# Marks in the model of a hand-planned order: the moves that hold a mark stop overwriting one another

## Chip, cores and metric

The kernel runs on one core of a Trainium2 chip. The metric is the device time of one execution in microseconds (us), the median of several runs.

## What is computed

Causal attention with a decay, for 8 batches of 8 heads with 576 positions and 64 columns per head, and then a two-layer MLP with a Mish gate over the 4608 tokens. Cut to what matters:

```
scores = q @ k.T / sqrt(64) + cum[:, None] - cum[None, :]    # cum = cumsum(log(clip(f)))
scores = where(causal, -1e9, scores)
attn   = softmax(scores) @ v                                 # (8, 8, 576, 64)
x      = attn as 4608 tokens x 512
h      = x @ w_in                                            # 512 -> 2048
out    = (h * tanh(softplus(h))) @ w_out                     # 2048 -> 512
```

## The kernel before

Every float32 value is carried as two float16 parts, high and low, and a product is made of several float16 products. The attention runs over 32 pairs of heads, g = 0 to 31, four pairs to a batch. The MLP runs over 9 chunks of 512 tokens; a chunk can start when the pairs of its batch are done. The weights are loaded as raw words and converted and split on the vector and scalar engines while the first pairs run.

For each pair g, `prep(g)` (line 1060) scales q and k, splits them into a tile `hl` with four parts (pairs 1 and 3 use a piece of `xa[1]` for it, line 1076), and issues DMAs that build the operand tile `ST1`. Two of them, one for t = 0 (the query side) and one for t = 1 (the key side), copy three rows for each of the two heads out of `cumd`, a DRAM tensor with the cumulative sums of the decay (line 1087); in the trace they are `st<-cumd`. They write different rows, D + 3t to D + 3t + 2, and different halves of the tile. Two more copy the high parts of q and k (line 1090); in the trace `st<-hl`, or `st<-xa` for pairs 1 and 3. `prep2(g)` (line 1094) fills the second operand tile `ST2` with four more copies of the same name. `max_items(g)` (line 1142) makes the scores a first time and takes row maxima with vector reductions into `mx`; `st_items(g)` makes them again for the exponentials.

Nothing is issued in the order in which the Python code runs. `Program.choose` (line 188) only records each operation, with the regions that it reads (`r`) and writes (`w`). `deps` (line 305) turns overlaps into a dependency graph: a write depends on earlier reads and writes of the region that it overlaps, a read on earlier writes. `schedule` (line 365) then runs a list scheduler with a cost model forward and backward ten times in all, replays each of the ten orders with four draws of random delays, and keeps the order with the lowest mean end. Some operations may go to one of several engines; the scheduler chooses (`choose` with several ways). `emit` writes each engine's instructions in that order. The real waits between engines are put in afterwards, from the tiles that the instructions touch, so the graph decides the order and the engines, not the synchronisation.

Beside true regions the graph has pretended ones. A *mark* is a pretended write: while `nc.mark` is set, each recorded operation also "writes" the region named by it. A *gate* is a pretended read: an operation recorded while `nc.gate` is set "reads" that region, and so comes after the operations that hold the mark. The marks are `rows0` to `rows3`, held by the two `st<-cumd` moves of pairs 0 to 3 (line 1085, `NSEL = 4`), and `sums`, held by the first store of `cumd` (line 796). The gates are `rows0` on the loads of all weights (line 883) and of the first batch of v (line 1795), and `rows2` on the second batch of v (line 1802). The q and k loads of pairs 2 and 3 carry the gate `rows0` as well (line 1764), but they are recorded ahead of the marks, so the marked moves come after them. In the model a DMA's successor becomes ready some 1.6 us after its issue cost, plus its bytes and a margin of 0.3 us (lines 592 to 596), and the SP queue, which issues nearly all DMAs, is held when the modelled backlog grows too long (line 523).

All marked moves write the same region of their mark:

```
if self.gate:
    r.append((self.gate, 0, 1, 0, 1))
if self.mark:
    w.append((self.mark, 0, 1, 0, 1))
```

The scheduler also fills some waits of the tensor engine with matmuls of no use, to keep its clock up (`warmed`, line 335); in the trace they are `b<-idm,idh`.

Of the kernel before, what the change touches and what calls it, by code (L numbers as in the profile page):

```python
# [27 lines left out]
S = 576  # L28
D = 64
# [100 lines left out]
BACK = 4000  # L130
LOOK = dict(zip(('tensor', 'vector', 'scalar', 'gpsimd', 'sync'), (float(x) for x in ("0", "0", "0", "0", "0",))))
PRIO = 200
MARGIN = dict(tensor=100,vector=100,scalar=100,gpsimd=0,sync=300)
DRAWS = 4
WORK, LAGS, MOVES = 0.02, 50.0, 300.0
# [25 lines left out]
class Program:  # L161
# [26 lines left out]
    def choose(self, *ways):  # L188

        r, w, opts = [], [], []  # L190
        for way in ways:
            total, port = 0.0, False
            for eng, method, a, kw in way:
                aps = [(k, x) for k, x in list(enumerate(a)) + list(kw.items()) if hasattr(x, "tensor")]
                w += [z for k, x in aps if k in ("out", "accum_out", 0) for z in self.region(x)]
                r += [z for k, x in aps if k not in ("out", "accum_out", 0) for z in self.region(x)]
                if eng == "scalar":
                    (r if method == "activation" else w).append(("table", 0, 1, 0, 1))
                if eng == "tensor":

                    w.append((w[0][0] + "/pe", 0, 1, 0, 1))
                port |= self.shared(eng, method, aps)
                cost = self.cost(eng, method, kw, aps)
                if isinstance(cost, tuple) and total:

                    total = (total[0] + 8, total[1] + cost[1], 0)
                else:
                    total = cost if isinstance(cost, tuple) else total + cost + (80 if total else 0)
            opts.append((eng, way, total, port))
        if self.gate:  # L210
            r.append((self.gate, 0, 1, 0, 1))
        if self.mark:
            w.append((self.mark, 0, 1, 0, 1))
        key = len(self.ops)
        if self.rank is not None:
            key, self.rank[1] = self.rank[0] + self.rank[1], self.rank[1] + self.rank[2]
        self.ops.append((opts, r, w, key))
        self.leads.append(self.lead)
        self.forms.append(self.form(*ways[0][0]) if ways[0][0][0] == "tensor" else None)
        func = ways[0][0][3].get("func") if ways[0][0][0] == "scalar" and len(ways) == 1 else None  # L220
        self.sets.append("mish" if func == AF.Mish else "exp" if func == AF.Exp else None)
        if self.sets[-1] and self.phase is not None:
            n = len(self.sets)
            w.append((f"phase{self.phase}", 0, 1, n, n + 1))
            r.append((f"phase{self.phase - 1}", 0, 1, 0, 1 << 30))

        self.banks.append({
            x.tensor.name for _, _, a, kw in ways[0] for x in list(a) + list(kw.values())
            if hasattr(x, "tensor") and x.space == PSUM})
# [248 lines left out]
    def forward(self, deps, succ, rank):  # L478
# [43 lines left out]
        while len(order) < n:  # L522
# [69 lines left out]
            if way[0][1].startswith("dma_start"):  # L592
                hw = max(t, hw) + cost[0]
                clock[q] = t + 50
                dma = max(dma, hw + 650) + cost[1]
                end, own = dma + 930 + MARGIN["sync"], 0.0
            else:
# [17 lines left out]
                clock[q] = t + cost  # L615
                end, own = clock[q], self.DELAY[q] + MARGIN[q]
            ends[i] = end
# [28 lines left out]
def scaled_rest(out, in_, scale, hi, e):  # L646

    if e == "vector":
        return [(e, "scalar_tensor_tensor", (), dict(
            out=out, in0=in_, scalar=scale, in1=hi, op0=ALU.mult, op1=ALU.subtract))]  # L650
    return scaled(in_, in_, scale, e) + sub(out, in_, hi, e)
# [32 lines left out]
def attn_moe(ctx: ExitStack, tc: tile.TileContext, qk, v, f, w_in, w_out, out):  # L684
    nc = Program(tc.nc)
# [26 lines left out]
        out=msk, in_=msk, pattern=[[-1, P]], compare_op=ALU.is_ge, fill=-60000.0,  # L712
# [4 lines left out]
    for j in range(2):  # L717
        nc.gpsimd.affine_select(
            out=msk2[j * D : (j + 1) * D], in_=msk2[j * D : (j + 1) * D], pattern=[[-1, D]],
# [14 lines left out]
    for j in range(2):  # L734
        r = slice(j * D, (j + 1) * D)
# [7 lines left out]
    ST1 = [cp.tile([P, 2, 2, S], F16, name=f"st1_{i}") for i in range(NST)]  # L743
    ST2 = [cp.tile([P, 2, 2, S], F16, name=f"st2_{i}") for i in range(NST2)]
# [3 lines left out]
    for t, first, fills in ((0, 0.0, ((KM - 4, -1.0), (KM - 1, 0.0))), (1, 1.0, ((KM - 4, 0.0), (MROW, -MSC), (KM, 0.0)))):  # L748
        nc.gpsimd.memset(rowv[:, t], first)
        for row, x in fills:  # L750
            nc.gpsimd.affine_select(
                out=rowv[:, t], in_=rowv[:, t], pattern=[[0, 2]], compare_op=ALU.is_ge, fill=x,
# [23 lines left out]
    def flat(t):  # L776
        return t[0:BH].rearrange("p j t s -> p (j t s)")

    tmp = [flat(ST2[i]).bitcast(F32)[:, S * j : S * (j + 1)] for i in (1, 0) for j in range(2)]
    ft = tmp[0]  # L780

    def decay():
        _, on, cm, r1 = tmp
        nc.vector.memset(on, 1.0)
        nc.vector.tensor_scalar(out=ft, in0=ft, scalar1=1e-4, scalar2=1.0, op0=ALU.max, op1=ALU.min)
        nc.scalar.activation(out=ft, in_=ft, func=AF.Ln)
        nc.scalar.preload_act_table_set("exp_and_others")
        nc.vector.tensor_tensor_scan(
            out=cm, data0=on, data1=ft, initial=0.0, op0=ALU.mult, op1=ALU.add)
        c = flat(ST2[1])[:, 0 : 3 * S].rearrange("p (r s) -> p r s", r=3)  # L790
        nc.vector.tensor_scalar(out=c[:, 0], in0=cm, scalar1=8.0, scalar2=None, op0=ALU.mult)
        nc.vector.scalar_tensor_tensor(
            out=r1, in0=cm, scalar=8.0, in1=c[:, 0], op0=ALU.mult, op1=ALU.subtract)
        nc.vector.tensor_copy(out=c[:, 1], in_=r1)
        nc.vector.tensor_tensor(out=c[:, 2], in0=r1, in1=c[:, 1], op=ALU.subtract)
        nc.mark = "sums"
        for h in (slice(0, H), slice(H, BH)):
            nc.mark = None if h.start else "sums"
            nc.sync.dma_start(out=cumd[h], in_=c[h])
        nc.mark = None  # L800
# [20 lines left out]
    def square_sum(o, x, scale=1.0):  # L821
        junk = sp.tile([P, S], BF16, name="junk", tag="junk", bufs=1)
        nc.scalar.activation(
            out=junk[:, 0 : x.shape[-1]], in_=x, func=AF.Square, scale=scale, accum_out=o)
# [232 lines left out]
    def place1(g):  # L1057
        return g % NST if g < NB else (g - NB + ((NB - 1) % NST == 0)) % 2

    def prep(g):  # L1060
        b, p = divmod(g, NP)
        x = st[g]["qk"]
        i = place1(g)
        am = sp.tile([P, 2], F32, name=f"qa{g}", tag="qa", bufs=4)
        for j in range(2):
            square_sum(am[:, j : j + 1], x[:, j])
        t = sp.tile([P, 2], F32, name=f"qt{g}", tag="qt", bufs=4)
        ami, ti = am.bitcast(I32), t.bitcast(I32)
        nc.vector.tensor_tensor(out=ti[:, 0:1], in0=ami[:, 1:2], in1=ami[:, 0:1], op=ALU.subtract)
        nc.vector.tensor_scalar(  # L1070
            out=ti[:, 0:1], in0=ti[:, 0:1], scalar1=0.25, scalar2=float(127 << 23), op0=ALU.mult, op1=ALU.add)
        nc.vector.tensor_scalar(
            out=ti[:, 0:1], in0=ti[:, 0:1], scalar1=EXPMASK, scalar2=None, op0=ALU.bitwise_and)
        nc.vector.reciprocal(out=t[:, 1:2], in_=t[:, 0:1])
        if g in (1, 3):
            hl = xa[1].rearrange("p a h n -> p (a h n)")[:, 0 : 4 * S].rearrange("p (t s) -> p t s", t=4)
        else:
            hl = sp.tile([P, 4, S], F16, name=f"hl{g}", tag="hl", bufs=NHL)
        for j, (hi, lo) in enumerate(((1, 3), (2, 0))):
            nc.choose(*(scaled(hl[:, hi], x[:, j], t[:, j : j + 1], e) for e in SV))  # L1080
            nc.choose(*(scaled_rest(hl[:, lo], x[:, j], t[:, j : j + 1], hl[:, hi], e) for e in (
                ("vector", "gpsimd") if AO & 2 else ("gpsimd",) if j < (HL2 if g < HLP else HL3) else ("vector",))))
        st[g]["hl"] = hl
        h0 = b * H + 2 * p
        nc.mark = f"rows{g}" if g < NSEL else None
        for t in range(2):
            nc.sync.dma_start(out=ST1[i][D + 3 * t : D + 3 * t + 3, :, t], in_=cumd[h0 : h0 + 2].rearrange("h r s -> r h s"))
        nc.mark = None
        for j in range(2):
            nc.sync.dma_start(out=ST1[i][0:D, j], in_=hl[j * D : (j + 1) * D, 1:3])  # L1090
        if NSEL <= g < NB and g - NST >= NSEL:
            nc.sync.dma_start(out=ST1[i][MROW : MROW + 1, :, 0], in_=zrow[0:1])
# [35 lines left out]
    def beside(*products):  # L1128
# [8 lines left out]
        out=sel, in0=idm[:, 0:9].unsqueeze(2).to_broadcast([P, 9, P]), scalar1=-MSC / 1024.0, scalar2=None,  # L1137
# [610 lines left out]
    def ranked(rank, f):  # L1748
# [8 lines left out]
        out=psum(RB)[:, 0:DN], lhsT=idh, rhs=idm.unsqueeze(1).to_broadcast([P, DN // P, P]), start=True, stop=True))]  # L1757
# [143 lines left out]
    for t0, t1 in zip([0] + TB, TB):  # L1901
        now = [place[x, t - x * W1] for t in range(t0, t1) for x in range(2) if 0 <= t - x * W1 < NF]
        for i in now:
            r = KS0 + i * KSS
# [92 lines left out]
```

## Time and profile before

| what | value |
|---|---|
| median of 3 runs | 1014.1 us (1013.09 to 1015.46) |
| the profiled execution: its own time | 1014.29 us |
| the profiled execution: span, first to last instruction | 1012.6 us |
| mean granted clock of the tensor engine | 0.993 |
| tensor engine busy | 978.1 us (97%) |
| vector engine busy | 731.1 us (72%) |
| scalar engine busy | 728.9 us (72%) |

A share over the whole span is a mean over stages with different limits, so it is read together with a table of the stages. In the trace all recorded operations have one line, 333, since one helper emits them; they are told apart by the names of their tiles. SPq is the queue of the engine SP that issues DMAs; PE is the tensor engine, PEld its weight loads, DVE the vector engine, ACT the scalar engine, POOL GpSimd.

### The profile page before, as it was taken

How to read it: one execution, taken by the hardware profiler on the slowest of the kernel's cores; microseconds unless marked ns; L12 is line 12 of the kernel's file. 1: busy time of each engine (PE TensorE's matmuls, PEld its weight loads, DVE VectorE, ACT ScalarE, POOL GpSimd, SP SyncE). 2: the span in 40 equal slices, each digit the busy share in tenths (PEclk: the TensorE clock that was granted, in tenths of full speed). 3: DMA queues.
4: the chain of work that ended last, by engine and by line, in shares of the span. 5: the costliest groups of instructions: out<-in, count | busy, mean ns of one | idle time of the engine just before them, and what ended most of it. 6: DMA issues, size and time to landing. Idle time of an engine off the chain costs nothing.

```text
span 1012.6 us, 20652 instructions
## 1 busy us (share of the span) xinstructions
PE 978.1 (97%) x7663; PEld 544.1 (54%) x7663; DVE 731.1 (72%) x2002; ACT 728.9 (72%) x1421; POOL 10.4 (1%) x65
## 2 busy tenths in 40 slices
PE   4999899998999999999999999999999999999998
PEld 4788445544554554555455555455555555656664
DVE  7999999986677776776666766776766669953432
ACT  6668999978778777777778877787886665524323
POOL 2000000000000000000000000000000000000000
PEclk8999999999999999999999999999999999999999
DMA  6999974779777857687868766786775432001001
GB/s 198 324 266 244 262 169 108 154 173 187 158 145 160 173 127 153 136 180 145 142 141 179 148 146 142 170 158 115 138 152 112 70 75 72 4 1 42 1 1 42
DMA packets 256446, 139.57 MB, mean 138 GB/s; under 512 B 226650, under 2 KB 227034, under 8 KB 256346
## 3 DMA queue, kind: packets, MB, share of 16 engines
q1 hardware_dynamic: 256346, 138.26, 61.7%
q8 instruction: 60, 0.98, 0.4%
q14 instruction: 40, 0.33, 0.1%
HBM read 45.68 MB, written 9.66 MB: 55 GB/s over the span
## 4 chain that ended last, share of the span: by engine, by line
PE 65%; DVE 16%; ACT 7%; DMA 6%; issue 3%; SPq 1%; POOL 0%; DVEq 0%; ACTq 0%; POOLq 0%
PE b L333 65%; DVE wall L333 3%; DVE b L333 2%; DMA pt<-hb 2%; DMA st<-hl 2%; SPq L333 1%; ACT junk L333 1%; DVE hl L333 1%; DVE hb L333 1%; ACT st L333 1%; ACT hb L333 1%; DMA out_dram<-ot 1%; DVE gl L333 1%; DVE x L333 1%; ACT more_e L333 1%
## 5 line engine op out<-in xcount | busy, mean ns | idle before, releaser
L333 PEld LDWEIGHTS <-wall 128*128 128x128 f16 x3372 | 322.3, 98 | 357.9 <-issue 24.0
L333 PE MATMUL b<-gh,wall 128*128 128x512 f16 x1152 | 366.5, 380 | 0.0
L333 PE MATMUL b<-xa,wall 128*128 128x512 f16 (+1 forms) x1602 | 345.0, 366 | 8.3 <-ACT me L333 4.6
L333 PE MATMUL b<-gl,wall 128*128 128x512 f16 x576 | 218.2, 379 | 0.6 <-DVE gl L333 0.6
L333 PE MATMUL b<-st 70*128 70x512 f16 (+11 forms) x918 | 139.1, 285 | 13.7 <-DMA st<-cumd 6.9
L333 DVE SCALAR_TENSOR_TENSOR gl<-me,gsc,gh 128x512 f16<-128x512 f32 x144 | 106.3, 748 | 32.6 <-ACT gh L333 31.7
L333 ACT ACTIVATE me<-b,cinv 128x512 f32<-128x512 f32 (+1 forms) x130 | 85.0, 660 | 56.6 <-PE b L333 55.7
L333 PEld LDWEIGHTS <-st 70*128 70x128 f16 (+3 forms) x1110 | 87.3, 102 | 63.6 <-issue 18.7
L333 PE MATMUL b<-vv,pt 128*128 128x65 f16 (+5 forms) x2548 | 111.7, 203 | 1.1 <-DMA pt<-hb 0.7
L333 DVE CUSTOM_DVE_ANT_0 b<-b,mskw 128x256 f32<-128x256 f32 (+2 forms) x162 | 91.6, 567 | 9.9 <-PE b L333 8.8
L333 ACT ACT_TABLE_LOAD x70 | 89.8, 1283 | 1.2
L333 PEld LDWEIGHTS <-pt 128*128 128x128 f16 (+1 forms) x2268 | 70.9, 101 | 19.3 <-DMA pt<-hb 2.3
L333 ACT ACTIVATE st<-b,mn 128x512 f32<-128x512 f32 (+3 forms) x120 | 62.1, 548 | 22.7 <-DVE mn L333 19.4
L333 DVE TENSOR_TENSOR hb<-st,hb 128x512 f16<-128x512 f32 x81 | 55.8, 689 | 29.6 <-ACT hb L333 29.1
L333 DVE TENSOR_TENSOR hb<-more_e,hb 128x512 f16<-128x512 f32 x81 | 55.5, 689 | 29.6 <-ACT hb L333 29.3
L333 ACT ACTIVATE more_e<-b,mn 128x512 f32<-128x512 f32 (+3 forms) x123 | 62.4, 539 | 17.3 <-DVE mn L333 15.8
L333 DVE TENSOR_SCALAR gh<-me,gsc 128x512 f16<-128x512 f32 x66 | 31.9, 483 | 45.2 <-ACT me L333 44.3
L333 ACT ACTIVATE gh<-me,gsc 128x512 f16<-128x512 f32 x78 | 55.8, 720 | 1.8
L333 ACT ACTIVATE hb<-more_e 128x512 f16<-128x512 f32 x81 | 50.1, 627 | 9.5 <-DMA pt<-hb 8.8
L333 ACT ACTIVATE hb<-st 128x512 f16<-128x512 f32 x81 | 50.2, 627 | 7.6 <-DMA pt<-hb 5.6
L333 DVE TENSOR_TENSOR me<-b,hb 128x256 f32<-128x256 f32 x42 | 17.5, 422 | 50.5 <-PE b L333 49.9
L333 ACT ACTIVATE junk<-qk 128x576 bf16<-128x576 f32 x60 | 40.8, 680 | 15.5 <-DMA qk<-in_qk_dram 14.8
(173 smaller groups left out, 1005.3 us busy)
## 6 DMA issues: line engine op xcount, KB each, us to landing
st<-hl SPq DMA_DIRECT2D x180, 144.0 KB
qk<-in_qk_dram SPq DMA_DIRECT2D x30, 576.0 KB
v<-in_v_dram SPq DMA_DIRECT2D x32, 288.0 KB
out_dram<-ot SPq DMA_DIRECT2D x36, 256.0 KB
wall<-in_w_in_dram SPq DMA_DIRECT2D x16, 512.0 KB
wall<-in_w_out_dram SPq DMA_DIRECT2D x16, 512.0 KB
pt<-hb SPq DMA_TRANSPOSE x162
st<-xa SPq DMA_DIRECT2D x12, 144.0 KB
```

Source lines behind the costliest of these rows:

```text
L333: r = getattr(real[eng], method)(*a, **kw)
```

## The change

A marked operation now writes a piece of the mark's region of its own, numbered by the operation, and a gated one reads the whole of it. So the operations that hold one mark no longer overlap: the t = 1 move of a pair no longer depends, in the model, on the t = 0 move. A gated operation still depends on every move that holds the mark and was recorded ahead of it, and a marked move still depends on gated loads recorded ahead of it. The rest of the diff has no effect as it stands: `NEAR` is 0, so the new branch is never taken, and `splits` is a view that was made in `decay` before. The recorded operations are the same.

```
+NEAR = 0
...
         if self.gate:
-            r.append((self.gate, 0, 1, 0, 1))
+            r.append((self.gate, 0, 1, 0, 1 << 30))
         if self.mark:
-            w.append((self.mark, 0, 1, 0, 1))
+            w.append((self.mark, 0, 1, len(self.ops), len(self.ops) + 1))
...
+    splits = flat(ST2[1])[:, 0 : 3 * S].rearrange("p (r s) -> p r s", r=3)
...
-        c = flat(ST2[1])[:, 0 : 3 * S].rearrange("p (r s) -> p r s", r=3)
+        c = splits
...
+            if g < NEAR:
+                for j in range(2):
+                    nc.sync.dma_start(out=ST1[i][D + 3 * t : D + 3 * t + 3, j, t], in_=splits[h0 + j : h0 + j + 1])
+                continue
```

## Rows read from the trace of the kernel before

**Rows 1.** The page's first part: busy time, share of the span and number of instructions of two engines.

```profile
PE 978.1 (97%) x7663; PEld 544.1 (54%) x7663; DVE 731.1 (72%) x2002; ACT 728.9 (72%) x1421; POOL 10.4 (1%) x65
```

**Rows 2.** Busy time by stage: the stretch in us, its length, then each engine's busy time and instructions, the granted clock of the tensor engine, the busy share of the DMA engines, and GB/s.

```profile
10.00:18.50 8.50, 1.57 (x29) 1.50 (x26) 6.75 (x24) 5.89 (x14) 0.00 (x0) 0.80 0.45 107
18.50:32.50 14.00, 10.68 (x93) 7.78 (x92) 10.70 (x27) 6.76 (x13) 0.00 (x0) 0.76 0.91 261
32.50:100.00 67.50, 66.12 (x743) 56.01 (x742) 66.62 (x191) 49.99 (x125) 1.05 (x5) 1.00 1.00 277
100.00:200.00 100.00, 94.89 (x702) 48.58 (x701) 99.02 (x287) 97.53 (x174) 0.81 (x4) 0.98 0.75 174
200.00:1000.00 800.00, 790.55 (x5999) 421.09 (x5997) 539.23 (x1463) 557.13 (x1078) 3.05 (x22) 1.00 0.58 119
1000.00:1012.60 12.60, 8.88 (x42) 3.82 (x39) 0.75 (x1) 3.18 (x5) 0.00 (x0) 0.96 0.22 83
```

**Rows 3.** The timeline of PE: start, length, operation, how many were merged, and in brackets the idle time before it with what ended it.

```profile
7.71 3.87 PE L333 MATMUL b<-idm,idh 128*128 128x128 f16 x62
18.51 0.27 PE L333 MATMUL b<-st 128*128 128x128 f16 x1 [6.94 <-DMA st<-cumd]
...
23.11 0.22 PE L333 MATMUL b<-st 128*128 128x128 f16 x1 [0.57 <-DVE mx L333]
...
27.95 0.23 PE L333 MATMUL b<-st 128*128 128x128 f16 x1 [1.87 <-DMA st<-xa]
```

**Rows 4.** The timeline of PEld: the first weight load of a score.

```profile
16.11 0.10 PEld L333 LDWEIGHTS <-st 128*128 128x128 f16 x1 [4.72 <-DMA st<-cumd]
```

**Rows 5.** The timeline of the SP queue from 12.5 us: start, length, the DMA that is issued.

```profile
12.99 1.13 SPq L333 DMA_DIRECT2D st<-hl  x2
14.22 1.05 SPq L333 DMA_DIRECT2D st<-cumd  x3
15.37 1.12 SPq L333 DMA_DIRECT2D st<-hl  x2
16.53 0.46 SPq L333 DMA_DIRECT2D st<-cumd  x1
17.03 1.88 SPq L333 DMA_DIRECT2D st<-hl  x2
18.96 0.46 SPq L333 DMA_DIRECT2D st<-cumd  x1
19.53 0.46 SPq L333 DMA_DIRECT2D st<-xa  x1
20.03 2.03 SPq L333 DMA_DIRECT2D v<-in_v_dram  x4
22.11 3.07 SPq L333 DMA_DIRECT2D st<-xa  x5
25.22 0.47 SPq L333 DMA_DIRECT2D st<-cumd  x1
26.05 1.62 SPq L333 DMA_DIRECT2D st<-hl  x2
27.92 1.88 SPq L333 DMA_DIRECT2D wall<-in_w_in_dram  x4
```

**Rows 6.** The same timeline asked for a narrow stretch (14.67 to 15.3 us): the second and the third of the three `st<-cumd` that are merged at 14.22.

```profile
14.67 0.60 SPq L333 DMA_DIRECT2D st<-cumd  x2
```

**Rows 7.** The timeline of DVE between 16 and 33 us.

```profile
16.65 1.55 DVE L333 SCALAR_TENSOR_TENSOR xa<-qk,qt,xa 128x576 f16<-128x576 f32 x2
19.56 1.35 DVE L333 TENSOR_REDUCE mx<-b 128x4 f32<-128x512 f32 x3 [1.36 <-PE b L333]
...
28.08 0.16 DVE L333 TENSOR_REDUCE am_m<-vc 128x1 f32<-128x4 f32 x1 [1.38 <-ACT junk L333]
...
32.45 0.42 DVE L333 TENSOR_SCALAR wall<-wall 128x512 int32<-128x512 int32 x1
```

**Rows 8.** The timeline of ACT.

```profile
20.63 1.44 ACT L333 ACTIVATE hl<-xa,qt 128x576 f16<-128x576 f32 x2 [4.01 <-DMA st<-hl]
23.21 0.68 ACT L333 ACTIVATE junk<-v 128x576 bf16<-128x576 f32 x1 [1.15 <-DMA v<-in_v_dram]
...
27.27 0.68 ACT L333 ACTIVATE junk<-v 128x576 bf16<-128x576 f32 x1 [0.43 <-DMA v<-in_v_dram]
```

**Rows 9.** The chain that ended last, in order of time: start, length, what the time went to.

```profile
22.11 5.80 DMA st<-xa
```

**Rows 10.** Busy time by stage again, for three stretches of the opening (columns as in rows 2).

```profile
14.50:18.50 4.00, 0.00 (x0) 0.10 (x1) 2.72 (x8) 1.52 (x3) 0.00 (x0) 0.57 0.67 153
18.50:22.50 4.00, 3.99 (x31) 2.98 (x30) 2.42 (x5) 1.44 (x2) 0.00 (x0) 0.58 0.68 171
22.50:32.50 10.00, 6.69 (x63) 4.80 (x62) 8.29 (x23) 5.32 (x11) 0.00 (x0) 0.83 1.00 297
```

**Rows 11.** Waits of PE from 100 us to the end: who waited for whom, us in total, times, the longest.

```profile
PE b L333 <- ACT me L333: 4.6, 5, 1.4
PE b L333 <- ACT st L333: 4.0, 7, 1.6
PE b L333 <- ACT more_e L333: 2.3, 3, 1.5
```

**Rows 12.** The page's costliest groups: operation and number | busy us, mean ns of one | idle before it. These are operations for which the scheduler may choose the engine.

```profile
L333 DVE SCALAR_TENSOR_TENSOR gl<-me,gsc,gh 128x512 f16<-128x512 f32 x144 | 106.3, 748 | 32.6 <-ACT gh L333 31.7
L333 DVE TENSOR_SCALAR gh<-me,gsc 128x512 f16<-128x512 f32 x66 | 31.9, 483 | 45.2 <-ACT me L333 44.3
L333 ACT ACTIVATE gh<-me,gsc 128x512 f16<-128x512 f32 x78 | 55.8, 720 | 1.8
```

## The prediction

> **What bounds the kernel now.** I read the shares first, then the table of stages, then the timelines of the opening. The tensor engine is busy for 97% of the span [rows 1], but the table of stages shows three regimes [rows 2]. From 200 to 1000 us PE is busy for 790.55 of 800 us: it is the bound. From 32.5 to 200 us DVE is busy for 66.62 of 67.5 and 99.02 of 100 us: DVE is the bound, with the DMA engines full beside it up to 100 us. Before 32.5 us nothing is full: from 10 us on DVE idles for 8.50 - 6.75 = 1.75 and 14.00 - 10.70 = 3.30 us, 5.05 us in all. A gain in the opening is worth what it takes out of those 5.05 us of DVE, because from there on DVE and then PE work without gaps, and all that follows shifts with them. It is worth no more.
>
> What the opening waits for stands in the timelines. PE makes fillers until 11.6 us and then idles for 6.94 us; its first score matmul starts at 18.51 us, and what ends the wait is a move `st<-cumd` [rows 3]. The weight load of that same matmul (the query side, t = 0) was let go at 16.11 us, also by an `st<-cumd` [rows 4]. So the two come from the two moves of pair 0: the first of the three issued at 14.22 us, 1.89 us ahead of the weight load, and the single one issued at 16.53 us, 1.98 us ahead of the matmul [rows 3 to 5]. Nothing on the chip parts them by 2.3 us: the queue issues without a longer pause in between, two other `st<-cumd` and two `st<-hl`. It is the planned order that puts t = 1 behind them, as the model has it wait for t = 0 to land.
>
> **The change, part by part.** Three edits (`NEAR`, `splits`, the untaken branch) issue nothing and cost nothing. What is left removes an edge between the two moves of each of pairs 0 to 3 and leaves the edges to the gated loads. No instruction is added and no wait on the chip; the queue SP issues the same DMAs in another order, and the rest of the order is planned anew.
>
> Pair 0. If the t = 1 move takes the place of the second of the three, it is issued at 14.67 us instead of 16.53 [rows 5, 6]: 1.86 us earlier. With the same 1.98 us to landing the first matmul starts at 16.65 us. The query and key copies of line 1090 are no new last wait: they were issued from 12.99 us on, and the weight load of 16.11 us had its half of them. What is late next is DVE: until 16.65 + 1.55 = 18.20 us it splits pair 1, and then it waits 1.36 us for the first scores [rows 7]. So of the 1.86 us DVE can take 1.36 us at this place, which is the whole wait. The clock of PE had fallen by then either way (granted 0.57 between 14.5 and 18.5 us, 0.58 in the next 4 us [rows 10], that is mostly the 1.2 GHz level), and DVE's reductions are the slower side, so I count nothing for it.
>
> The gated loads. The four v loads are issued at 20.03 us [rows 5], after the last mark of `rows0` has landed in the model. With that landing 1.86 us earlier they may be planned up to 1.86 us earlier. They carry the next wait: the sums of squares of v on ACT wait three times for them, the last time at 27.27 us, and DVE waits 1.38 us for these until 28.08 us [rows 7, 8]. The nearest bound on what the loads can gain is the idle time of the DMA engines ahead of the full stretch: 4 x (1 - 0.67) + 4 x (1 - 0.68) = 2.6 us between 14.5 and 22.5 us [rows 10]; at the other end it is nothing, or a loss if the loads pass copies that are more urgent. I take the shift of the gate, 1.86 us, since it is the nearest row: then the wait at 28.08 us moves by 1.86 us, 0.5 us more than the DVE gained before it, and DVE's first weight conversion, at 32.45 us, comes 1.9 us earlier. The bounds of this sum are 0 and 5.05 us, the idle time of DVE above.
>
> SP. The queue issues from 12.99 us almost without a pause, some 0.35 to 0.6 us per DMA and once nearly 1.4 us for a pair's last copy [rows 5]. What moves up pushes something back. Moving one `st<-cumd` ahead of the two `st<-hl` delays these by 0.46 us, and if all six moves of pairs 0 to 2 go to the front, the last `st<-hl` are delayed by one more, 0.46 us; ACT waits for the last of them until 20.63 us, to overwrite their source with pair 2 [rows 8]. Pair 2's scores aren't wanted before those of pair 1, so up to 0.9 us there costs nothing; the cover is the wait for pair 1 below.
>
> Pairs 1 to 3. Pair 1's first scores at 23.11 us end a wait of 0.57 us for a reduction, not for a move, and its second head waits until 27.95 us for `st<-xa` [rows 3]. Pair 2's second move (25.22 us) is followed by its `st<-hl` at 26.05 us [rows 5], which land later. Pair 3 lies in the stretch where DVE is full. I count nothing for the three.
>
> A rule against the change: the copy `st<-xa` that ends the wait at 27.95 us was issued at 22.11 us, right behind the four v loads, and took 5.80 us [rows 9], where the small moves ahead of the loads took 1.9 to 2.0 us [rows 3 to 5]. So a copy that gets behind the loads pays some 3.9 us. [...] By that rule loads that move up take their shift out of every copy that they pass, and the 1.9 us could come to nothing; that is the second rival below.
>
> The rest of the order. The scheduler plans everything anew from changed start times, and none of this can be read from the trace. Its bound on the side of a gain is the idle time of PE after 100 us, 5.11 + 9.45 + 3.72 = 18.3 us [rows 2], of which the longest group of waits has 4.6 us [rows 11]. On the side of a loss I take the same size. As the value I take nothing, since no row gives it a sign.
>
> The sum: 1014.29 us of the profiled execution less 1.9 us is 1012.4 us. That execution lies 0.19 us above the median of the runs, so against the median, 1014.1 us, the forecast is 1012.2 us.
>
> **The rivals.** First, slower: the new plan gives DVE more of the work that may go to either engine, in the stretch where DVE is full. Between 100 and 200 us DVE has 99.02 and ACT 97.53 of 100 us [rows 2], so neither has room, and one more low part there costs DVE 0.75 us, one more high part 0.48 us [rows 12]. Nine more of one kind and of the other alike, at 0.6 us in the mean, cost 5.4 us less the 1.9 us gained: 1017.6 us. It decides from 3.2 us more (the gain is eaten) and counts as slower from 1.9 + 2.0 = 3.9 us, six or seven operations. For it speaks that in 100 us nothing hides them; against it that the scheduler weighs the same engines as before.
>
> Second, no change: the v loads are planned ahead of both `st<-xa` of pair 1, or the t = 1 move stays where it is because the chosen one of ten orders has other moves first. In the first case pair 1's first head, issued at 19.53 us just ahead of the loads [rows 5], pays the 3.9 us of the second. It would land near 19.53 + 1.98 + 3.9 = 25.4 us, DVE would run out of pair 0's reductions, and the 1.36 us would be lost there: 1014.1 us. For it speaks that the loads stand one place behind that copy; against it that loads which start earlier also end earlier.
>
> Third, much faster: the new order also closes a third of the waits behind 100 us, about 5 us of 18.3 us: 1012.2 - 5 = 1007.2 us. For it speaks that the waits of PE on ACT there are many and short, 15 of 0.7 us in the mean [rows 11]; against it that PE is already at 98.8% from 200 us on [rows 2].
>
> **How the numbers follow.** About 0.2% of the time, 2.0 us, is what a measurement of this kernel can tell from no change, so the bounds are 1012.1 and 1016.1 us. The forecast has 0.42, and as it lies at the bound, half of it, 0.21, is faster and half the same. Slower has 0.27, no change 0.13, much faster 0.18. Faster: 0.21 + 0.18 = 0.39. Same: 0.21 + 0.12 = 0.33. Slower: 0.27 + 0.01 = 0.28. The likeliest case's own range is 1009.9 to 1014.1 us. The range reaches to the greater part of both outer cases, from 1007.0 to 1018.0 us, and leaves out a tenth at either end.
>
> **What would show it.** Right: the first score matmul starts near 16.65 us after a wait of about 5 us, two `st<-cumd` adjacent before it; DVE has no wait above 1 us for it; v loads issued near 18.2 us; the first weight conversion near 30.6 us; the stages after 200 us the same but for the shift. Wrong: the first matmul early and the conversion still at 32.4 us (second rival); more DVE instructions between 32.5 and 200 us and PE's idle time there above 6 us (first); or a total that differs by several us while the opening gains its 2 us, which would say that the re-planned rest decides and not the edge.

## The result, and the profile after

The changed kernel is slower: 1021.28 us (median of 4 runs, 1019.19 to 1021.58) against 1013.6 us of the kernel before in the same session, a ratio of 1.0068 with a 95% interval of 1.0049 to 1.0088 (the two medians by themselves would give 1.0076). The profiled execution took 1021.53 us; its span is 1019.8 us, 7.2 us more than before. The forecast was 1012.2 us and its range ended at 1018.0 us.

The opening answers to [rows 3 to 9]. The timeline of PE of the changed kernel (start, length, operation, idle time before it and what ended that):

```profile
15.21 0.27 PE L334 MATMUL b<-st 128*128 128x128 f16 x1 [5.44 <-DMA st<-cumd]
...
26.87 0.22 PE L334 MATMUL b<-st 128*128 128x128 f16 x1 [4.08 <-DMA st<-cumd]
```

The timeline of its SP queue:

```profile
11.94 1.13 SPq L334 DMA_DIRECT2D st<-hl  x2
13.17 1.36 SPq L334 DMA_DIRECT2D st<-cumd  x4
14.57 2.39 SPq L334 DMA_DIRECT2D st<-hl  x4
17.01 2.46 SPq L334 DMA_DIRECT2D v<-in_v_dram  x4
19.58 3.89 SPq L334 DMA_DIRECT2D st<-xa  x6
24.72 1.76 SPq L334 DMA_DIRECT2D st<-cumd  x2
```

The timeline of its DVE:

```profile
16.90 3.80 DVE L334 TENSOR_REDUCE mx<-b 128x4 f32<-128x512 f32 x8
20.81 1.54 DVE L334 SCALAR_TENSOR_TENSOR hl<-xa,qt,hl 128x576 f16<-128x576 f32 x2
27.09 0.16 DVE L334 TENSOR_REDUCE am_m<-vc 128x1 f32<-128x4 f32 x1 [4.74 <-ACT junk L334]
...
32.99 0.42 DVE L334 TENSOR_SCALAR wall<-wall 128x512 int32<-128x512 int32 x1
```

The timeline of its ACT, the sums of squares of the first and the last v load:

```profile
21.35 0.67 ACT L334 ACTIVATE junk<-v 128x576 bf16<-128x576 f32 x1
...
26.28 0.68 ACT L334 ACTIVATE junk<-v 128x576 bf16<-128x576 f32 x1 [0.72 <-DMA v<-in_v_dram]
```

The reader is to see three things. The removed edge did what was meant: the two moves of pair 0 now stand side by side, and the first score matmul starts at 15.21 us, 3.30 us earlier than before. (More than the 1.86 us of the move, since the work ahead of it was planned anew too: the first `st<-hl` goes out at 11.94 us instead of 12.99.) The four v loads went ahead of both copies `st<-xa` of pair 1. And by the first weight conversion the gain is gone: DVE, which had no wait for the first scores any more, waits 4.74 us for the sums of squares of v, PE waits 4.08 us for pair 1, and the conversion starts at 32.99 us instead of 32.45 us [rows 7]. PE's line names `st<-cumd` as what ended its wait; the moves at 24.72 us belong to pair 2. What pair 1 needed besides is the two copies behind the loads, which is tested below.

The stages answer to [rows 2] (columns as there), and the pace of the kernel shows in the output stores. The stages of the changed kernel:

```profile
10.00:18.50 8.50, 3.29 (x25) 2.69 (x26) 7.83 (x27) 4.65 (x11) 0.00 (x0) 0.75 0.58 136
18.50:32.50 14.00, 9.33 (x87) 6.92 (x88) 8.48 (x23) 6.58 (x14) 0.10 (x1) 0.74 0.88 240
32.50:100.00 67.50, 65.42 (x735) 55.39 (x732) 66.11 (x187) 50.53 (x121) 0.48 (x4) 0.98 0.88 263
100.00:200.00 100.00, 93.74 (x667) 48.75 (x666) 98.81 (x285) 97.16 (x174) 0.42 (x3) 0.98 0.78 180
200.00:1000.00 800.00, 788.62 (x6023) 419.17 (x6022) 541.88 (x1474) 553.53 (x1059) 3.19 (x23) 1.00 0.58 120
```

Two groups of output stores of the kernel before, from the timeline of its SP queue:

```profile
323.49 1.01 SPq L333 DMA_DIRECT2D out_dram<-ot  x2
...
929.09 5.15 SPq L333 DMA_DIRECT2D out_dram<-ot  x4
```

The same two of the changed kernel:

```profile
326.89 1.01 SPq L334 DMA_DIRECT2D out_dram<-ot  x2
...
936.03 5.15 SPq L334 DMA_DIRECT2D out_dram<-ot  x4
```

In these two executions the changed kernel is 0.54 us late at its first weight conversion, 3.4 us late at the stores near 325 us, 6.9 us late at those near 930 us and 7.2 us at the end. So most of the loss shows far behind the opening, where the change is. This doesn't yet say where it arises: each trace is one execution, and the experiments show how far two executions of one order lie apart. Nor need it arise where the plans differ: between the 4332nd and the 8084th operation (some 400 to 760 us) both plans have the same order and the same engines, and there the lateness grows from 3.33 us (stores at 549.72 instead of 546.39 us) to 4.82 us (at 645.31 instead of 640.49 us).

DVE and ACT changed too. The page's parts of the changed kernel, busy time and costliest groups (columns as in [rows 1, 12]):

```profile
PE 981.4 (96%) x7677; PEld 546.1 (54%) x7677; DVE 736.8 (72%) x2018; ACT 728.0 (71%) x1403; POOL 9.1 (1%) x65
...
L334 DVE TENSOR_SCALAR gh<-me,gsc 128x512 f16<-128x512 f32 x69 | 33.1, 483 | 47.8 <-ACT me L334 47.0
```

DVE has 16 instructions and 5.7 us more than before, ACT 18 instructions fewer [rows 1]; three of DVE's are high parts of the gate (69 instead of 66 [rows 12]). In the two plans 66 of the 1004 operations that may go to either engine went to another one, so "instructions unchanged" holds for the recorded operations only; 14 more fillers on PE came with it.

### The profile page after: what moved, and what is told of

Read it like the earlier page. It is cut to its first block, busy times and chain, and to the rows that moved or that the text cites. A ratio compares the mean times of both kernels' runs of the same rounds, so it can differ in the third digit from the quotient of the medians.

```text
span 1019.8 us, 20694 instructions
## 1 busy us (share of the span) xinstructions
PE 981.4 (96%) x7677; PEld 546.1 (54%) x7677; DVE 736.8 (72%) x2018; ACT 728.0 (71%) x1403; POOL 9.1 (1%) x65
## 4 chain that ended last, share of the span: by engine, by line
PE 62%; DVE 16%; ACT 9%; DMA 7%; issue 4%; SPq 2%; ACTq 0%; DVEq 0%
PE b L334 62%; DVE wall L334 3%; DVE b L334 3%; DMA st<-hl 2%; SPq L334 2%; DMA qk<-in_qk_dram 2%; DVE hb L334 2%; DMA pt<-hb 2%; DVE hl L334 1%; ACT hb L334 1%; ACT st L334 1%; DVE gl L334 1%; ACT junk L334 1%; ACT more_e L334 1%; DVE xp L334 1%
## 5 line engine op out<-in xcount | busy, mean ns | idle before, releaser
L334 DVE CUSTOM_DVE_ANT_0 b<-b,mskw 128x256 f32<-128x256 f32 (+2 forms) x162 | 91.3, 566 | 13.7 <-PE b L334 12.5
L334 ACT ACTIVATE gh<-me,gsc 128x512 f16<-128x512 f32 x75 | 53.7, 719 | 1.8
```

The lines of the kernel that those rows point to most:

```text
L334: r = getattr(real[eng], method)(*a, **kw)
```

## The experiments

All kernels record the same operations as the changed one; what differs is the order in which they are emitted. The edits are given in short form, not as the code stands: `a` is the order of the kernel before, `b` that of the changed kernel, each with its engines. Ratios are against the kernel before in the same session, with 95% intervals; 0.1% is 1.0 us.

**The move alone.**

```diff
+order = a
+first, second = (the two operations that hold the mark rows0)
+order.remove((second, 0))
+order.insert(order.index((first, 0)) + 1, (second, 0))
```

> The order planned for the kernel before, but the t = 1 move of pair 0 is issued right behind its t = 0 move; every other instruction on every queue keeps its place. The theory (the change's loss comes from the newly planned rest of the order, not from the move) expects the first score matmul near 16.65 us and 1.0 to 1.9 us less than before, about 1012 us. The rival (moving the row copies early is itself harmful, since it pushes back the copies of ST2 and what follows) expects the first matmul early and yet no gain, or a loss of a few us.

Measured: 0.9987 (0.9967 to 1.0007), with medians of 1015.66 and 1015.63 us. The timeline of PE of this kernel, then that of its DVE:

```profile
16.27 0.26 PE L343 MATMUL b<-st 128*128 128x128 f16 x1 [4.92 <-DMA st<-cumd]
...
28.81 0.29 PE L343 MATMUL b<-st 128*128 128x128 f16 x1 [2.72 <-DMA st<-xa]
```

```profile
20.94 0.82 DVE L343 SCALAR_TENSOR_TENSOR hl<-xa,qt,hl 128x576 f16<-128x576 f32 x1 [1.48 <-ACT hl L343]
...
29.06 0.16 DVE L343 TENSOR_REDUCE am_m<-vc 128x1 f32<-128x4 f32 x1 [2.86 <-ACT junk L343]
...
33.80 0.42 DVE L343 TENSOR_SCALAR wall<-wall 128x512 int32<-128x512 int32 x1
```

The DVE instruction of the first of these lines in the kernel before:

```profile
21.44 0.82 DVE L333 SCALAR_TENSOR_TENSOR hl<-xa,qt,hl 128x576 f16<-128x576 f32 x1 [0.52 <-ACT hl L333]
```

The first matmul is 2.24 us early, somewhat more than expected. DVE's wait of 1.36 us for the first scores is gone, but its next wait, for ACT's part of pair 2's `hl`, grows from 0.52 to 1.48 us, so only 0.50 us is left at 20.94 us; at the wait for the v sums (2.86 us instead of 1.38) and at the first conversion nothing is. The move by itself is harmless, and its gain of 1.3 us isn't clear of nothing. That the loss comes from the move is refuted.

This trace also shows how little one execution says of where a kernel loses time. Its busy time in the second stage (columns as in [rows 2]), then its stores near 325 us:

```profile
18.50:32.50 14.00, 9.33 (x63) 6.13 (x61) 9.13 (x21) 6.03 (x13) 0.00 (x0) 0.50 0.91 244
```

```profile
327.00 1.01 SPq L343 DMA_DIRECT2D out_dram<-ot  x2
```

The stores are as late as those of the changed kernel (326.89 us), though the median of this kernel is that of the kernel before. In the execution that was traced (1017.53 us; the twelve ran from 1012.30 to 1019.52 us) PE had the 1.2 GHz level (granted 0.50) from 18.5 to 32.5 us, where the trace before has 0.76.

**Parts of the two orders joined.** At 217, 4332 and 8084 operations both orders have done the same set, so one can be followed up to there and the other from there on.

```diff
+cuts = 217, 4332, 8084
+order = b[:217] + a[217:]                            # new opening
+order = a[:217] + b[217:4332] + a[4332:]             # new middle
+order = a[:8084] + b[8084:]                          # new end
+order = b[:4332] + a[4332:]                          # opening and middle
```

> The recorded operations fall into the same sets in both planned orders at three places: before the first weight conversion (217 operations), after 4332 and after 8084 operations. Here the first 217 operations (to about 33 us) are in the order of the changed kernel, all the rest in that of the kernel before. The theory (most of the loss lies behind the opening) expects 0 to 1 us more than before, since the first weight conversion of the changed kernel is 0.5 us late in its trace. The rival (the v loads that pass pair 1's copies cause the loss, and all else follows from it) expects 6 to 8 us more.

Measured: 1.0050 (1.0030 to 1.0070).

> Operations 218 to 4332 (about 33 to 400 us, of which those up to 3567, some 325 us, differ) in the order of the changed kernel, the opening and the rest as before. The theory expects about 3 us more than before (the changed trace is 0.5 us late at 33 us and 3.4 us late at its third pair of output stores, near 325 us). The rival that puts all on the opening expects no more than 0.5 us either way.

Measured: 1.0063 (1.0047 to 1.0080).

> Operations 8085 to the end (about 760 us on) in the order of the changed kernel, all before it as before. The theory expects about 2 us more than before (the changed trace is 4 to 5 us late near 760 us and 7 us late at its end). The rival that puts all on the opening expects no difference.

Measured: 1.0018 (1.0000 to 1.0035).

> The first 4332 operations in the order and on the engines of the changed kernel, the rest as before. The new opening alone cost 5 us and the new middle alone 6.4 us, and the changed kernel as a whole 6.9 us. If each part pays for the seam with a part of the other order, the two together cost no more than 5 us (6.9 less the 1.8 us of the new end). If the two costs belong to the parts themselves they add up to 11 us.

Measured: 1.0047 (1.0029 to 1.0066).

The new opening alone costs 5 us, not 0 to 1; so does the new opening with the new middle, 4.7 us; and the new middle behind the old opening costs 6.3 us, twice what was expected. The new end, 1.8 us, is as expected. The costs of the parts don't add up: 5.0 + 6.3 = 11.3 us against 4.7 us. A likely reason is the seam: a part was planned for a state of queues and engines that the other order doesn't leave. The traces don't show it. Between 100 and 200 us, where DVE is the bound, DVE is busy for less time with the new middle behind the old opening than in either whole order (98.81 us in the changed kernel, 99.02 us in the kernel before [rows 2]). But it is busy for as little in the kernel with opening and middle, which has the order of the changed kernel up to the 4332nd operation and no seam before it. The busy time by stage of the new middle alone, then that of opening and middle:

```profile
100.00:200.00 100.00, 92.14 (x628) 47.89 (x627) 96.21 (x277) 94.27 (x167) 0.41 (x3) 0.97 0.76 175
```

```profile
100.00:200.00 100.00, 92.35 (x649) 47.60 (x648) 96.22 (x275) 94.72 (x166) 0.50 (x3) 0.97 0.76 175
```

So two executions of one order differ by 2.6 us in this stage. The same holds in the opening. The first weight conversion, from the timelines of DVE, in the two kernels with the old opening (new middle, new end):

```profile
32.67 0.42 DVE L354 TENSOR_SCALAR wall<-wall 128x512 int32<-128x512 int32 x1
```

```profile
33.07 0.42 DVE L354 TENSOR_SCALAR wall<-wall 128x512 int32<-128x512 int32 x1
```

And in the two with the new opening (new opening alone, opening and middle):

```profile
33.72 0.42 DVE L354 TENSOR_SCALAR wall<-wall 128x512 int32<-128x512 int32 x1
```

```profile
31.94 0.42 DVE L354 TENSOR_SCALAR wall<-wall 128x512 int32<-128x512 int32 x1
```

With the kernel before (32.45 us) and the changed one (32.99 us), three traces of the old opening lie between 32.45 and 33.07 us and three of the new one between 31.94 and 33.72 us. The new opening doesn't reach that point 1.9 us earlier, and its 0.54 us of lateness in the changed trace is within the scatter.

So these kernels say that the first 4332 operations hold some 5 us and the last 2449 perhaps 2, and they can't share out the 5 us between opening and middle.

**Order and engines parted.**

```diff
+order = [(i, engine of i in a) for i in b]     # new order, old engines
+order = [(i, engine of i in b) for i in a]     # old order, new engines
```

> The order of the changed kernel, but each operation that may go to one of several engines goes where the kernel before has it (66 of 1004 differ). In the changed trace DVE is busy 5.7 us longer, by 16 instructions. If work moved to DVE where DVE is full makes the loss, this is 3 to 5 us faster than the changed kernel, so 2 to 4 us slower than before. If the order makes it, it stays 6 to 8 us slower than before.

Measured: 1.0162 (1.0139 to 1.0185). Outside both expectations, like the next.

> The reverse: the order of the kernel before, the engines of the changed kernel for the 66 operations. If work moved to DVE makes the loss, 3 to 5 us slower than before. If the order makes it, within 2 us of before; but any set of engines that doesn't belong to its order may cost something by itself.

Measured: 1.0123 (1.0098 to 1.0148).

Either mix is far worse than both whole plans. In the first, DVE is busy for only 88.81 us between 100 and 200 us, by the stages:

```profile
100.00:200.00 100.00, 88.08 (x598) 45.95 (x598) 88.81 (x255) 94.75 (x167) 0.46 (x3) 0.95 0.71 165
```

The work moved to DVE can't be blamed by itself: taking it back in the new order costs 16 us against before, more than twice the loss. In these two plans an order fits only its own engines. What the moved work costs inside its own order stays untested.

**The loads that pass the copies.** The kernel with the move alone, and one step more on SP in either direction.

```diff
+order = (the move alone), then
+order: the four v loads before the first st<-xa copy of pair 1
+order: or the second st<-xa copy of pair 1 before the four v loads
```

> As the kernel with only the t = 1 move put forward, but the four v loads too are issued ahead of the first st<-xa copy of pair 1, as the changed kernel has them; all else in the order of the kernel before. If the loads that pass the copies are what makes the new opening dear (it cost 5 us in front of the old rest), this costs 3 to 5 us against the kernel before, with a wait of PE and DVE of 2 us or more near 23 to 27 us. If they are harmless and the rest of the opening's order counts, it stays within 1.5 us of the kernel with the move alone (about 1.3 us faster than before).

Measured: 1.0021 (1.0001 to 1.0042), 3.4 us above the move alone (1.0021 - 0.9987). Its timeline of SP, then those of PE and DVE:

```profile
21.30 3.69 SPq L349 DMA_DIRECT2D st<-xa  x6
```

```profile
26.98 0.26 PE L349 MATMUL b<-st 128*128 128x128 f16 x1 [6.71 <-DMA st<-xa]
```

```profile
28.02 0.69 DVE L349 TENSOR_REDUCE mx<-b 128x4 f32<-128x512 f32 x1 [3.76 <-PE b L349]
```

PE waits 6.71 us for pair 1's copies, until 26.98 us, where PE's wait of the changed kernel's opening ends too (26.87 us); this one step brings it about. DVE's 3.76 us are a wait for these scores, where DVE of the changed kernel waits for the v sums. The expectation of 3 to 5 us against before was too high (2.1 us). Against the kernel with the move alone it holds, but barely: the two were timed in different sessions, and with about 2 us to either side for each, the difference is 3.4 us with about 2.9 us to either side. The two traced executions took the same time (1017.35 and 1017.53 us), so they don't show where it arises.

> The order of the kernel before with the t = 1 move of pair 0 right behind its t = 0 move, and the second st<-xa copy of pair 1 ahead of the four v loads instead of behind them (it took 5.8 us there); all else as before. If that copy is what keeps the early move from paying, PE's wait near 28 us goes and this is 2 to 3 us faster than before. If the v loads themselves set the pace (DVE waits for the sums of squares of v until 28 to 29 us), they come half a us later and this is no faster than before, within 1.5 us.

Measured: 1.0033 (1.0009 to 1.0057): slower, which neither expectation had. Its timeline of SP, then those of PE and DVE:

```profile
19.19 1.10 SPq L350 DMA_DIRECT2D st<-xa  x2
```

```profile
22.34 0.22 PE L350 MATMUL b<-st 128*128 128x128 f16 x1 [2.02 <-DMA st<-xa]
```

```profile
29.61 0.16 DVE L350 TENSOR_REDUCE am_m<-vc 128x1 f32<-128x4 f32 x1 [3.68 <-ACT junk L350]
...
33.49 0.42 DVE L350 TENSOR_SCALAR wall<-wall 128x512 int32<-128x512 int32 x1
```

The second copy no longer waits, but the v loads are issued 0.4 us later and the wait for their sums ends at 29.61 us. Copies and loads go through one queue (q1 of the page), and in these two kernels whichever went first made the other the last wait. Why the total grew by 3.3 us isn't settled. The trace can't show it: its execution took 1014.48 us, about as long as the traced one of the kernel before (1014.29 us). The twelve executions ran from 1012.70 to 1024.51 us, and the loss goes with the mean granted clock of PE: its median is 0.989, against 0.993 of the kernel before in that session, and the two longest executions had 0.984 and 0.985, the shortest 0.997. What lowers it isn't shown.

**New plans that mean nothing.** One number of the model, the margin behind a DMA, is changed by a nanosecond or two, with the edges of the kernel before or with those of the changed kernel.

```diff
-MARGIN = dict(tensor=100,vector=100,scalar=100,gpsimd=0,sync=300)
+MARGIN = dict(tensor=100,vector=100,scalar=100,gpsimd=0,sync=299)    # or 301, 298, 302
+order = plan(old edges)    # or plan(new edges)
```

> The graph of the kernel before, with all its edges between marked moves, planned again with one number of the model changed by a nanosecond: the margin behind a DMA is 299 instead of 300. This changes nothing that means anything, and gives another order. If the loss of the changed kernel is what any new plan costs against this one order, this one moves by several us too, most likely to the slower side (3 to 10 us). If the loss belongs to the removed edges, it stays within 2 us of before.

> The same with a margin of 301. The same two expectations: several us, most likely slower, or within 2 us.

> The old edges, planned with a margin of 298. If any new plan costs several us against this one order, whatever its edges: 2 to 10 us slower than before, and the mean of the plans with old edges within 2 us of that of the plans with new ones. If the removed edges cost something of their own, the plans with old edges (now four with before) stay 2.5 us or more below those with new ones in the mean.

> The old edges, planned with a margin of 302. The same two expectations as for 298.

> The graph of the changed kernel planned with a margin of 299. If any new plan scatters, this lies somewhere between 2 us faster and 12 us slower than before and needn't lie near the changed kernel. If the removed edges cost what they seem to, it lies 5 to 9 us slower, as the changed kernel does.

> The graph of the changed kernel planned with a margin of 301. The same two expectations as for 299: anywhere between 2 us faster and 12 us slower, or 5 to 9 us slower.

> The new edges, planned with a margin of 298. If scatter alone decides, anywhere from 0 to 12 us slower than before, in the mean of the five such plans within 2 us of those with old edges. If the removed edges cost something of their own (their plans all put the v loads ahead of both copies of pair 1), 6 to 9 us slower, as the three so far.

> The new edges, planned with a margin of 302. The same two expectations as for 298.

| margin | old edges | new edges |
|---|---|---|
| 298 | 1.0059 (1.0041 to 1.0077) | 1.0026 (1.0010 to 1.0042) |
| 299 | 1.0073 (1.0056 to 1.0089) | 1.0071 (1.0056 to 1.0085) |
| 300 | 1 (the kernel before) | 1.0068 (1.0049 to 1.0088) (the changed kernel) |
| 301 | 1.0032 (1.0015 to 1.0049) | 1.0092 (1.0072 to 1.0112) |
| 302 | 1.0024 (1.0001 to 1.0048) | 1.0086 (1.0062 to 1.0111) |

All four plans with the old edges are slower than the kernel before, by 2.4 to 7.3 us, for a change that means nothing; two of them by as much as the changed kernel, within the intervals. Their mean is 0.47% (4.7 us). The five plans with the new edges have a mean of 0.69%; the one with 298 lies below the 6 to 9 us that edges with a cost of their own were to show. The plan with the old edges and the margin of 299 keeps the opening of before (a late first matmul, one copy ahead of the loads). In the stretch where DVE is full DVE is busy for 2.5 us less than before, which is no more than two executions of one order can differ there. Its timeline of PE, then its busy time between 100 and 200 us:

```profile
18.07 0.27 PE L340 MATMUL b<-st 128*128 128x128 f16 x1 [7.17 <-DMA st<-cumd]
```

```profile
100.00:200.00 100.00, 90.45 (x648) 46.27 (x647) 96.53 (x283) 94.22 (x162) 0.41 (x3) 1.00 0.73 168
```

So a loss of this size needs neither the removed edges nor the new opening. Whether the edges add something is less clear. The means differ by 0.22% without the kernel before and by 0.31% with it among the old ones; the single plans scatter by 0.23 and 0.26% (standard deviations of the four and the five), which leaves 0.16% of uncertainty on the difference of 0.22%. By the bound that was set ahead (2.5 us, with before) the edges cost about 3 us of their own, the size of what the loads ahead of the copies cost; but this is under two of its uncertainties (0.22 against 0.16%), so it is possible and not shown.

**Only pair 0's edge.**

```diff
-order = plan(new edges)
+order = plan(old edges for rows1, rows2 and rows3, the new one for rows0)
```

> Only the edge between the two moves of pair 0 is removed; the three other pairs keep theirs; planned anew. Its plan too puts the v loads ahead of both copies of pair 1. If the early gate of the loads adds to what a new plan costs: 5 to 9 us slower than before, as the plans with all edges removed. If scatter alone decides: anywhere from 0 to 12 us.

Measured: 1.0034 (1.0012 to 1.0056), below the 5 to 9 us that the early gate was to show. It too puts the loads ahead of both copies, and DVE waits 4.00 us for the v sums. One more plan within the scatter of all the others.

## Why the prediction was wrong

**What bounds the kernel:** right that DVE and then PE are nearly full behind 32.5 us (66.11 of 67.5, 98.81 of 100, 788.62 of 800 us in the changed trace). That all behind the opening shifts with it isn't borne out in full. The stores of the kernel with the loads ahead, near 325 and 535 us, behind which it has the order of before:

```profile
328.70 1.01 SPq L349 DMA_DIRECT2D out_dram<-ot  x2
...
538.45 0.56 SPq L349 DMA_DIRECT2D out_dram<-ot  x1
```

The second of these stores in the kernel before:

```profile
535.27 0.58 SPq L333 DMA_DIRECT2D out_dram<-ot  x1
```

It is 5.21 us late at the first (323.49 us before) and 3.18 us at the second: 2 us of lateness were taken up on the way.

**Pair 0's move:** right in mechanism. Side by side on SP, 1.86 us expected for the move and 2.24 us measured with the move alone; DVE's wait of 1.36 us for the first scores is gone in both traces.

**The gated loads:** this step failed, as the second rival said, in the opening. The sum let the v loads land 1.86 us earlier; they were issued 3.0 us earlier (17.01 instead of 20.03 us), and the last of their squares starts only 1.0 us earlier (26.28 instead of 27.27 us), while the two copies of pair 1 fell behind them. The 2.6 us of idle time of the DMA engines was taken for room. The changed kernel's busy time between 16 and 20 us (columns as in [rows 2]):

```profile
16.00:20.00 4.00, 4.00 (x31) 2.99 (x29) 4.00 (x9) 0.00 (x1) 0.00 (x0) 0.50 0.97 239
```

The DMA engines are 97% busy there. The wait for v took the place of the wait for the first scores, and the first conversion came no earlier: at 31.94 to 33.72 us in three traces of the new opening, 32.45 to 33.07 us in three of the old one, where the sum had 1.9 us. That a copy behind the loads pays was borne out, with a price below the 3.9 us: those compared copies of 144 KB with moves of 6.8 KB. Of pair 1's copies, the first one behind the loads took 5.7 us until its scores started (21.30 to 26.98 us), the one ahead of them in the kernel with move and copy 3.15 us (19.19 to 22.34 us).

**SP and pairs 1 to 3:** wrong, for the move alone, that ACT's wait for the copies of `ST2`, to overwrite their source with pair 2, costs nothing: DVE waits 1.48 us for ACT's part behind it, and most of the 1.36 us gained goes there. In the changed kernel it costs nothing, as DVE's new order puts five more reductions ahead of that instruction and it starts at 20.81 us without a wait. Wrong too that pair 1 had nothing at stake, as its first copy was in front of the loads before.

**The rest of the order:** the step that made the forecast wrong. "As the value I take nothing, since no row gives it a sign" put 0 us where the runs show 2.4 to 7.3 us for plans with the old edges, a mean of 4.7 us, and always the same sign. The size stood in the bound (18.3 us), and the range didn't use it: its upper end came from another mechanism. All ten other plans of the same work that were timed are slower than the kernel before (four with old edges, five with new ones, one with pair 0's edge alone). That its order is the survivor of many tries would explain this, but no run can show how it was found. What is shown is that plans which differ by one or two nanoseconds in one number of the model lie up to 0.7% apart on the chip.

**The first rival** (more work on DVE) named the right side and a thing that happened, 16 instructions and 5.7 us more on DVE. Its cause isn't shown: in the full stretch up to 200 us DVE ran 472 instructions instead of 478, and giving the work back made the kernel slower still. Its sign, PE idle for more than 6 us between 32.5 and 200 us, could not have told, since the kernel before idles there for 1.38 + 5.11 = 6.49 us [rows 2]. **The third rival** (shorter waits later) went the other way: PE idles 6.26 us instead of 5.11 between 100 and 200 us and 11.4 instead of 9.45 us up to 1000 us.

Left open: how the 5 us of the first 4332 operations divide between opening and middle, since the costs of the joined orders don't add up; and whether the removed edges cost 2 to 3 us of their own. Also open is PE's clock. The kernel before has a median of its mean granted clock of 0.993 in every later session, the changed kernel 0.991 and the eight plans with another margin 0.9885 to 0.992, so a part of what a new plan costs may go with it; not all, as the kernel with only pair 0's edge has 0.993 and loses 3.4 us. No run parts the two. No kernel tried was faster than the kernel before clear of its interval.

## What to carry to other kernels

Where a list scheduler orders the work, a change to its model is two changes: the one that is meant, which can be tried alone by moving that one instruction in the old order, and a new draw of everything else. Measure the draw first, by changing a number that means nothing, and take its mean and scatter into the forecast; here the order in hand beat all ten new ones. When a wait in front of a full engine is removed, look for the next wait and for what the same edge lets through the queue: here loads that were held back by the late move passed the copies that came next.

## What the runs showed that I had not expected

Loads that were issued 3.0 us earlier, onto busy DMA engines, were all there only 1.0 us earlier. In the changed kernel the engines were 96% busy at 200 GB/s while v loads and copies between tiles were in flight (first row, 22.5 to 26.5 us); in the kernel before they reached 410 GB/s at 102% where mostly weight loads ran (second row, 32 to 36 us). So a busy share of the DMA engines says little about bytes. What sets the rate isn't shown: from 22.5 to 26.5 us the kernel before moved 313 GB/s at 102%, with v loads and copies too.

```profile
22.50:26.50 4.00, 0.29 (x6) 0.12 (x3) 0.00 (x0) 1.70 (x5) 0.00 (x0) 1.00 0.96 200
```

```profile
32.00:36.00 4.00, 3.96 (x60) 3.20 (x58) 3.86 (x10) 1.95 (x7) 0.24 (x1) 0.99 1.02 410
```

The kernel before itself had medians of 1013.6 to 1016.3 us in the six sessions; ratios within one session are what can be compared.
